# Block 0's first-layer products from unsplit float32 weights and tokens, with the weights split afterwards for block 1

## The chip, the cores and the metric

The kernel runs on one core of one Trainium2 chip. Its time is the device time of one execution in microseconds (us), and versions are compared by the median of several runs on the same chip. The engines carry the names of the profile: PE is TensorE's matmul, PEld its weight load, DVE is VectorE, ACT is ScalarE, POOL is GpSimd, and SP is SyncE, which issues most of the transfers.

## The reference, cut to what matters

Three layers follow one another over 4608 tokens of 512 numbers. The first is attention with 8 batches, 8 heads, 576 queries and keys and values averaged in groups of 8. The second, called the max layer here, is

```python
h = np.maximum(np.maximum(x @ w1, x @ w2), x @ w3)   # 512 -> 768, three weights
y = h @ w_out                                        # 768 -> 512
```

and the third is `h = np.maximum(y @ w_in, 0); out = (h * h) @ w_out` with 2048 hidden units. Everything is float32.

## The kernel before

**Precision.** A float32 operand is written as a sum of two numbers of the type that the profile prints as fp32r, a high part and a low part. `split` makes them: ACT copies the source into the high part (line 135), and a second engine, DVE unless POOL is named, subtracts that from the source and writes the low part (line 136). A product then takes three matmuls for each 128 rows, in the order of `PARTS`: high by high, high by low, low by high. Where an operand is plain float32 the kernel passes it to one matmul as it is; attention does so for the scores (line 367), and for the batch that `NATURAL` counts, batch 0, also for pooling v (line 270) and for the product of probabilities and values (line 426).

**Weights.** The weights come as 64-bit numbers, 512 KB for each 128 by 512 tile. `load_raw` fetches such a tile, `convert` makes float32 bits of it with two ACT instructions (lines 162 and 163) and two DVE instructions (lines 164 and 167) in a tile of the tag `row`, which has three buffers, and `split` with POOL makes the two parts. `weights` does all of it. The max layer has 18 such tiles for its first half (6 slices `f` of the hidden units, 3 weights `e`) and 6 for its second (`wo1`).

**Blocks.** The tokens are taken in 12 blocks of 384. A block of the max layer is 22 steps: 18 products of the first half, four times three matmuls each, and four of the second half. A step yields after its instructions are written down. Attention for block j+1 runs beside the max layer of block j, and attention for blocks 0 and 1 and the preparation of all 24 weight tiles share the start of the kernel. In block 1 the six products of the first `AHEAD` = 2 slices are placed between block 0's last four steps.

**Order.** Everything is put in a list `todo` with a due time in steps, and `run` writes it down in the order of these times. That order gives instructions their priority; a scheduler then fixes each engine's order. An engine takes its instructions strictly in that order. `ps` has three PSUM banks, `hm` (the running maximum) two buffers.

**After block 0.** The second layer's weights are converted and split during blocks 2 to 11, and the third layer follows. None of its code is touched.

Of the kernel before, what the change touches and what calls it, by code (L numbers as in the profile page):

```python
# [11 lines left out]
F32R = mybir.dt.float32r  # L12
I32 = mybir.dt.int32
U32 = mybir.dt.uint32
AF = mybir.ActivationFunctionType
ALU = mybir.AluOpType
# [4 lines left out]
P = 128  # L21
# [6 lines left out]
KD = DM // P  # L28
FF1 = 768
KF1 = FF1 // P  # L30
FF2 = 2048
KF2 = FF2 // P
NE = 3
# [7 lines left out]
PARTS = ((0, 0), (0, 1), (1, 0))  # L41
# [22 lines left out]
AHEAD = 2  # L64
# [21 lines left out]
def as_f32(ap):  # L86
    return ap.bitcast(F32)
# [8 lines left out]
def attention_moe_kernel(ctx: ExitStack, tc: tile.TileContext, q, k, v, vn, w1, w2, w3, wo1, wi2, wo2, out):  # L96
    nc = tc.nc
# [11 lines left out]
    for sign, base in ((1, POOL * MID), (-1, POOL - 1 - POOL * MID)):  # L109
        nc.gpsimd.affine_select(  # L110
            out=sums, in_=sums, compare_op=ALU.is_ge, fill=0.0, base=base,
# [15 lines left out]
    def place(kind):  # L127
        if shared[0]:
            turns["both"] += 1
            return f"raw{turns['both'] % 4}"  # L130
        turns[kind] += 1
        return f"raw{2 * kind + turns[kind] % 2}"

    def split_to(hi, lo, src, engine):
        nc.scalar.activation(hi, src, AF.Copy)  # L135
        engine.tensor_tensor(out=lo, in0=src, in1=as_f32(hi), op=ALU.subtract)  # L136

    def split(hl, src, engine=nc.vector):

        split_to(hl[:, 0], hl[:, 1], src, engine)  # L140

    def load_raw(raw_pool, src, after=None):

        raw = raw_pool.tile([P, 512, 2], I32, tag=place(0), name="wraw", bufs=1)
        if after is not None:
            nc.gpsimd.tensor_copy(as_f32(raw[:1, 0, :1]), after[:1, :1])
        nc.sync.dma_start(out=raw.rearrange("p a b -> p (a b)"), in_=src.bitcast(I32))
        return raw

    def convert(raw_pool, raw, after=None):  # L150

        low, high = raw[:, :, 0], raw[:, :, 1]
        a = raw_pool.tile([P, 512], I32, tag="row", name="wbits", bufs=3)
        if after is not None:  # L160
            nc.gpsimd.tensor_copy(as_f32(a[:1, :1]), after[:1, :1])
        nc.scalar.activation(as_f32(a), as_f32(high), AF.Abs, scale=REBIAS)
        nc.scalar.activation(low, low.bitcast(U32), AF.Copy, scale=LOW_SCALE, bias=LOW_BIAS)  # L163
        nc.vector.scalar_tensor_tensor(
            out=a, in0=a, scalar=3, in1=low, op0=ALU.logical_shift_left, op1=ALU.bitwise_or
        )
        nc.vector.scalar_tensor_tensor(
            out=a, in0=high, scalar=-0x80000000, in1=a, op0=ALU.bitwise_and, op1=ALU.bitwise_or
        )
        return as_f32(a)  # L170

    def in_place(raw):
        return raw.rearrange("p a b -> p (a b)").rearrange("p (c a) -> p c a", c=2).bitcast(F32R)
# [1 line left out]
    def weights(pool, raw_pool, src, name, tag=None):  # L175
        w = pool.tile([P, 2, 512], F32R, name=name, tag=tag or name)
        split(w, convert(raw_pool, load_raw(raw_pool, src)), nc.gpsimd)
        return w


    w_p = s1.enter_context(tc.tile_pool(name="w_p", bufs=1))
# [6 lines left out]
    raw_p = s_at.enter_context(tc.tile_pool(name="raw_p", bufs=4, side="right"))  # L188
# [143 lines left out]
    def attend(j, b, s0, n, p, t):  # L332
# [86 lines left out]
        def values():  # L419
            if t == 0:  # L420
                x_t[j][p] = x_p.tile([P, 2, T1], F32R, tag="x", name="x")
            x = x_t[j][p][:, :, t : t + n]
            if whole:
                av = av_ps.tile([P, T1], F32, tag="av0", name="av0")[:, :n]
                for h in range(2):
                    nc.tensor.matmul(
                        av, lhsT=vst_f[p // 2][:, p % 2, h : h + 2].rearrange("p a d -> p (a d)"), rhs=pt[0][:, h, :n],
                        start=(h == 0), stop=(h == 1),
                    )
                split(x, av)  # L430
                return
            hi, lo = pt[0][:, 0, :, :n], pt[0][:, 1, :, :n]
            xf = xf_p.tile([P, T1], F32, tag="xf", name="xf")[:, :n]
            for h in range(2):
                av = av_ps.tile([P, T1], F32, tag=f"av{h}", name=f"av{h}")[:, :n]
                lhsT = vst[:, p, 2 * h : 2 * h + 2].rearrange("p a d -> p (a d)")
                nc.tensor.matmul(av, lhsT=lhsT, rhs=hi[:, h], start=True, stop=False)  # L437
                nc.tensor.matmul(av, lhsT=lhsT, rhs=lo[:, h], start=False, stop=True)  # L438
                r, o = slice(h * D, (h + 1) * D), slice((1 - h) * D, (2 - h) * D)
                nc.scalar.activation(xf[r], av[o], AF.Copy)  # L440
                nc.vector.tensor_tensor(out=xf[r], in0=av[r], in1=xf[r], op=ALU.add)  # L441
            split(x, xf)

        return load, prepare, softmax, carry, transpose, values

    w1_t, wo1_t = {}, {}

    def load_w1(f, e):
        w1_t[f, e] = weights(w_p, raw_p, (w1, w2, w3)[e][f], f"w1_{f}_{e}")

    def load_second(src, raw):
        raw.append(load_raw(raw_p, src, now[0]))
# [4 lines left out]
    def prepare_out(raw, rows, f):  # L457
# [4 lines left out]
        def store(m, hi, lo):  # L462
            for i, w in enumerate((hi, lo)):
                store_second(wo2_dram[m, g, h][:, u, i], w)

        rows.append(convert(raw_p, raw[0], now[0]))
        own = in_place(raw[0])
        l, r = slice(0, 256), slice(256, 512)
# [58 lines left out]
    now = [None]  # L527

    def moe1(j):

        x = x_t.pop(j)
        hs = []
        for f in range(KF1):
            hm = t_p.tile([P, T1], F32, tag="hm", name="hm")
            h = (ah_p if j == 1 and f < AHEAD else h_p).tile([P, 2, T1], F32R, tag="h", name="h")
            for e in range(NE):
                ps = mm_ps.tile([P, T1], F32, tag="ps", name="ps")
                n = 0
                for kk in range(KD):
                    for a, c in PARTS:  # L540
                        nc.tensor.matmul(  # L541
                            ps, lhsT=w1_t[f, e][:, a, kk * P : (kk + 1) * P], rhs=x[kk][:, c],
                            start=(n == 0), stop=(n == 3 * KD - 1),
                        )
                        n += 1
                if e == 0:
                    nc.scalar.activation(hm, ps, AF.Copy)
                else:
                    nc.vector.tensor_tensor(out=hm, in0=ps, in1=hm, op=ALU.max)  # L549
                if e == NE - 1:  # L550
                    split(h, hm)
                yield
            hs.append(h)
            now[0] = hm
        for d in range(KD):
            ps = mm_ps.tile([P, T1], F32, tag="ps", name="ps")
            n = 0
            for kk in range(KF1):
                for a, c in PARTS:
                    nc.tensor.matmul(  # L560
                        ps, lhsT=wo1_t[kk][:, a, d * P : (d + 1) * P], rhs=hs[kk][:, c],
                        start=(n == 0), stop=(n == 3 * KF1 - 1),
                    )
                    n += 1
            ys = t_p.tile([P, T1], F32, tag="ys", name="ys")
            nc.scalar.activation(ys, ps, AF.Copy)
            nc.scalar.dma_start(out=y_dram[j][d], in_=ys)
            yield
# [6 lines left out]
    def add_moe1(j):  # L575
        steps = moe1(j)
        for i in range(STEPS):
            when = j * STEPS + i
            if j == 1 and i < NE * AHEAD:
                when = NE * KF1 + i * KD / (NE * AHEAD)  # L580
            todo.append((when, functools.partial(next, steps, None)))

    todo = []
    attention(0)
    for f in range(KF1):
        for e in range(NE):
            todo.append((0.9 * (NE * f + e) - 12, functools.partial(load_w1, f, e)))
    for kk in range(KF1):
        todo.append((0.9 * (NE * KF1 + kk) - 12, functools.partial(load_wo1, kk)))
    for j in range(NB1 - 1):  # L590
        add_moe1(j)
        attention(j + 1)

    second = []
    for f in range(0, KF2, 2):
        rows = []
        for i in (f, f + 1):
            raw = []
            second.append((wi2[i], raw, functools.partial(prepare_in, raw, rows, i)))
        rows = []  # L600
        for i in (f // 2 + KF2 // 2, f // 2):
            raw = []
            second.append((wo2[i], raw, functools.partial(prepare_out, raw, rows, i)))
    for i, (src, raw, prepare) in enumerate(second):
        when = STEPS * (SECOND[0] + (i + 0.5) * (SECOND[1] - SECOND[0]) / len(second))
# [236 lines left out]
    for j in range(NB2):  # L842
        for gr in range(NG):
            more = j + 1 < NB2
            c = moe2_in(j, gr)
# [55 lines left out]
```

## Time and profile before

| | |
|---|---|
| median of 3 runs | 1461.22 us (1458.98 to 1462.27) |
| time of the profiled execution | 1462.14 us |
| its span | 1459.7 us |
| PE busy | 1425.5 us, 98% |
| DVE busy | 977.9 us, 67% |
| ACT busy | 759.4 us, 52% |
| POOL busy | 182.9 us, 13% |

The span is the stretch that the trace covers; the 2.4 us around it belong to the time and not to the trace. Busy times are sums over the whole span and hide how unlike its parts are. Only the first 8% or so of the span concerns block 0, and the rows below are therefore taken by stretch. The ends of matmuls are modelled, so PE counts as busy where matmuls follow each other loosely too.

### The profile page before, as it was taken

The numbers are of one execution on the slowest core, as the hardware profiler recorded it, in microseconds if no ns is written. First come the engines' busy times: TensorE is split into PE (matmuls) and PEld (weight loads), VectorE is DVE, ScalarE is ACT, GpSimd is POOL, SyncE is SP. The second block draws the span as 40 slices with busy tenths as digits, with TensorE's granted clock in tenths as the row PEclk, the third lists the DMA queues.
The fourth block names the chain that finished last, engine by engine and source line by source line (L and its number), as shares of the span: only waits on it lengthen the run. The fifth ranks groups of instructions, "written<-read, shape, count | busy, mean of one in ns | idle before, by whom it ended". The sixth has DMA issues, their size and how long they took to land.

```text
span 1459.7 us, 27670 instructions
## 1 busy us (share of the span) xinstructions
PE 1425.5 (98%) x10410; PEld 1403.0 (96%) x10410; DVE 977.9 (67%) x1754; ACT 759.4 (52%) x1959; POOL 182.9 (13%) x229
## 2 busy tenths in 40 slices
PE   6889999999999999999999999999999999999998
PEld 4879999999999999999999999999999999999998
DVE  5887477656675756646336767686867767686865
ACT  7795366655665657655223544453535444454543
POOL 3441022212322222221000000000000000000000
PEclk9989999999999999999999999999999999999999
DMA  7554145444455444433459747566566666555746
GB/s 226 182 169 141 62 143 180 162 140 142 146 180 177 149 148 142 133 120 107 167 190 355 290 160 256 186 223 222 209 221 224 232 231 221 204 217 199 258 153 209
DMA packets 125029, 272.81 MB, mean 187 GB/s; under 512 B 13504, under 2 KB 69568, under 8 KB 124896
## 3 DMA queue, kind: packets, MB, share of 16 engines
q1 hardware_dynamic: 117984, 261.61, 52.8%
q10 hardware_dynamic: 6912, 9.44, 1.8%
q8 instruction: 82, 1.34, 0.4%
q14 instruction: 51, 0.42, 0.1%
HBM read 213.91 MB, written 48.23 MB: 180 GB/s over the span
## 4 chain that ended last, share of the span: by engine, by line
PE 77%; DMA 5%; DVE 2%; ACT 1%; issue 1%; SPq 0%; POOL 0%; ACTq 0%; DVEq 0%; POOLq 0%
PE ps L701 23%; PE ps L541 22%; PE ps L560 8%; PE accB L825 6%; PE accA L825 6%; PE accE L825 3%; PE accF L825 3%; DMA wo2s<-wo_dram 3%; PE accD L825 2%; PE sc L367 2%; PE av L438 1%; PE av L437 1%; DMA wraw<-in_wi_dram 0%; PE tr L408 0%; DMA yr<-y_dram 0%
## 5 line engine op out<-in xcount | busy, mean ns | idle before, releaser
L541 PE MATMUL ps<-x,w 128*128 128x384 f32 x2592 | 491.0, 342 | 5.5 <-ACT w L135 3.0
L541 PEld LDWEIGHTS ps<-x,w 128*128 128x128 f32 x2592 | 452.0, 190 | 8.3 <-ACT w L135 3.4
L701 PE MATMUL ps<-y,wi2s 128*128 128x256 f32 x3024 | 372.8, 278 | 0.7 <-DVE a L672 0.2
L701 PEld LDWEIGHTS ps<-y,wi2s 128*128 128x128 f32 x3024 | 357.2, 188 | 2.4 <-DVE c L672 1.3
L560 PE MATMUL ps<-h,wo 128*128 128x384 f32 x864 | 159.0, 337 | 0.1
L560 PEld LDWEIGHTS ps<-h,wo 128*128 128x128 f32 x864 | 149.6, 188 | 0.3 <-ACT wo L135 0.2
L714 ACT ACTIVATE c<-c 128x512 f32<-128x512 f32 x90 | 56.3, 626 | 168.6 <-DVE c L672 168.0
L672 DVE TENSOR_TENSOR c<-ps,c 128x512 f32<-128x512 f32 x144 | 98.2, 687 | 66.4 <-PE ps L701 63.5
L549 DVE TENSOR_TENSOR hm<-ps,hm 128x384 f32<-128x384 f32 x144 | 79.7, 553 | 81.3 <-PE ps L541 78.8
L135 ACT ACTIVATE g<-c 128x512 fp32r<-128x512 f32 x144 | 90.3, 627 | 57.0 <-DVE c L711 23.3
L825 PE MATMUL accA<-wo2s,g 128*128 128x256 f32 x864 | 115.6, 277 | 0.0
L825 PE MATMUL accB<-wo2s,g 128*128 128x256 f32 x864 | 111.7, 279 | 3.9 <-DMA wo2s<-wo_dram 3.0
L372 ACT ACTIVATE ss<-sc,st 128x72 f32<-128x72 f32 (+1 forms) x320 | 97.8, 320 | 29.9 <-DVE st L369 24.8
L825 PEld LDWEIGHTS accB<-wo2s,g 128*128 128x128 f32 x864 | 104.5, 189 | 4.9 <-ACT g L135 2.2
L136 DVE TENSOR_TENSOR g<-c,g 128x512 fp32r<-128x512 f32 x144 | 97.8, 686 | 16.4 <-ACT g L135 16.4
L825 PEld LDWEIGHTS accA<-wo2s,g 128*128 128x128 f32 x864 | 107.0, 188 | 0.0
L441 DVE TENSOR_TENSOR xf<-av,xf 64x192 f32<-64x192 f32 (+1 forms) x112 | 50.7, 452 | 39.3 <-ACT xf L440 37.6
L378 POOL TENSOR_TENSOR ss<-ss,st 128x432 f32<-128x432 f32 (+1 forms) x64 | 53.1, 830 | 178.3 <-DVE st L377 95.0
L135 ACT ACTIVATE h<-hm 128x384 fp32r<-128x384 f32 x72 | 37.6, 522 | 56.2 <-DVE hm L549 55.5
L372 ACT ACTIVATION_READ_ACCUMULATOR ss<-sc,st 128x1 f32 (+1 forms) x320 | 66.2, 207 | 0.0
L135 ACT ACTIVATE g<-s 128x512 fp32r<-128x512 f32 x72 | 44.3, 630 | 35.3 <-DVE s L675 17.5
L163 ACT ACTIVATE wraw<-wraw 128x512 int32<-128x512 uint32 x56 | 37.8, 675 | 43.4 <-DMA wraw<-in_wi_dram 16.4
(111 smaller groups left out, 1929.2 us busy)
## 6 DMA issues: line engine op xcount, KB each, us to landing
wo2s<-wo_dram SPq DMA_DIRECT2D x252, 512.0 KB, 5.8
wi2s<-wi_dram SPq DMA_DIRECT2D x24, 512.0 KB, 6.5
wraw<-in_wo_dram SPq DMA_DIRECT2D x22, 512.0 KB, 3.9
wraw<-in_w_dram SPq DMA_DIRECT2D x18, 512.0 KB, 5.2
y_dram<-ys ACTq DMA_DIRECT2D x48, 192.0 KB, 2.7
wraw<-in_wi_dram SPq DMA_DIRECT2D x16, 512.0 KB, 3.7
wi_dram<-wraw SPq DMA_DIRECT2D x16, 512.0 KB, 3.0
wo_dram<-wraw SPq DMA_DIRECT2D x64, 128.0 KB, 2.1
```

The source lines that it names most:

```text
L135: nc.scalar.activation(hi, src, AF.Copy)
L136: engine.tensor_tensor(out=lo, in0=src, in1=as_f32(hi), op=ALU.subtract)
L372: nc.scalar.activation(ss[:, i, h], src[:, i, h], AF.Exp, bias=st[:, 0, i, h : h + 1], accum_out=st[:, 1, i, h : h + 1],)
L378: nc.gpsimd.tensor_tensor(out=ss, in0=ss, in1=st[:, 2].rearrange("p g (h o) -> p g h o", o=1).to_broadcast([m, g, 2, SP]), op=ALU.mult,)
L441: nc.vector.tensor_tensor(out=xf[r], in0=av[r], in1=xf[r], op=ALU.add)
L541: nc.tensor.matmul(ps, lhsT=w1_t[f, e][:, a, kk * P : (kk + 1) * P], rhs=x[kk][:, c], start=(n == 0), stop=(n == 3 * KD - 1),)
L549: nc.vector.tensor_tensor(out=hm, in0=ps, in1=hm, op=ALU.max)
L560: nc.tensor.matmul(ps, lhsT=wo1_t[kk][:, a, d * P : (d + 1) * P], rhs=hs[kk][:, c], start=(n == 0), stop=(n == 3 * KF1 - 1),)
L672: nc.vector.tensor_tensor(out=out, in0=in0, in1=in1, op=ALU.add)
L701: nc.tensor.matmul(bank[:, u * HT : (u + 1) * HT], lhsT=wi2_t[2 * gr + u][i][:, a, o + kk * P : o + (kk + 1) * P], rhs=y_t[j][m][:, c, kk] ...
L714: nc.scalar.activation(c, c, AF.Relu)
L825: nc.tensor.matmul(bank[:, i * 256 : (i + 1) * 256], lhsT=g[:, a, u * HT + i * P : u * HT + (i + 1) * P], rhs=w[:, u, c], start=(n == 0 an ...
```

## The change

For block 0 the first half of the max layer is computed with one float32 matmul for each 128 rows, from the converted weights and the unsplit tokens. Block 0's tokens are therefore written once, as float32, by ACT; their subtraction on DVE goes. The converted weight goes straight to a place of its own: two weights share one tile of the size that a split weight has, from the tag `w1_17` downwards, and the last one stays in the `row` buffer. `split_w1` makes the two parts later. It is due behind step 15 for the six weights of the slices 0 and 1, with DVE for the subtraction, and behind step 18 for the other twelve, with POOL. It starts with a copy of one number from the newest `hm` into the target, on POOL, so that the split can't run before that `hm` is final. The targets of the weights 9 to 17 are the tiles that held the unsplit pairs.

```diff
-    def convert(raw_pool, raw, after=None):
+    def convert(raw_pool, raw, after=None, out=None):
...
+        if out is None:
+            out = a
         nc.vector.scalar_tensor_tensor(
-            out=a, in0=high, scalar=-0x80000000, in1=a, op0=ALU.bitwise_and, op1=ALU.bitwise_or
+            out=out, in0=high, scalar=-0x80000000, in1=a, op0=ALU.bitwise_and, op1=ALU.bitwise_or
         )
-        return as_f32(a)
+        return as_f32(out)
...
-                split(x, av)
+                if j == 0:
+                    nc.scalar.activation(as_f32(x[:, 0]), av, AF.Copy)
+                else:
+                    split(x, av)
...
     def load_w1(f, e):
-        w1_t[f, e] = weights(w_p, raw_p, (w1, w2, w3)[e][f], f"w1_{f}_{e}")
+        i = NE * f + e
+        if i == LAST:
+            dst = None
+        else:
+            if i % 2 == 0:
+                two[0] = w_p.tile([P, 2, 512], I32, tag=f"w1_{LAST - i // 2}", name="wf")
+            dst = two[0][:, i % 2]
+        raw = load_raw(raw_p, (w1, w2, w3)[e][f])
+        wf_t[f, e] = convert(raw_p, raw, out=dst)
+
+    def split_w1(f, e):
+        i = NE * f + e
+        half = LAST // 2
+        w1_t[f, e] = w_p.tile([P, 2, 512], F32R, tag=f"w1_{i if i <= half else LAST + half + 1 - i}", name=f"w1_{f}_{e}")
+        nc.gpsimd.tensor_copy(w1_t[f, e][:1, 0, :1], now[0][:1, :1])
+        split(w1_t[f, e], wf_t.pop((f, e)), nc.vector if f < AHEAD else nc.gpsimd)
...
-                    for a, c in PARTS:
-                        nc.tensor.matmul(
-                            ps, lhsT=w1_t[f, e][:, a, kk * P : (kk + 1) * P], rhs=x[kk][:, c],
-                            start=(n == 0), stop=(n == 3 * KD - 1),
-                        )
+                    for a, c in parts:
+                        cols = slice(kk * P, (kk + 1) * P)
+                        if j == 0:
+                            lhsT, rhs = wf_t[f, e][:, cols], as_f32(x[kk][:, c])
+                        else:
+                            lhsT, rhs = w1_t[f, e][:, a, cols], x[kk][:, c]
+                        nc.tensor.matmul(ps, lhsT=lhsT, rhs=rhs, start=(n == 0), stop=(n == len(parts) * KD - 1))
                         n += 1
...
+    for f in range(KF1):
+        for e in range(NE):
+            i = NE * f + e
+            when = NE * (KF1 - 1) if f < AHEAD else NE * KF1
+            todo.append((when + 0.05 * (i + 1), functools.partial(split_w1, f, e)))
```

## Rows read from the trace of the kernel before

**Rows 1.** Busy time of each engine by stretch, granted clock (PEclk, 1.00 is 2.4 GHz).

```profile
28.00:50.00 22.00, 16.36 (x81) 13.20 (x81) 16.80 (x36) 17.47 (x65) 9.33 (x9) 0.88 0.66 194
50.00:75.00 25.00, 24.61 (x153) 23.50 (x152) 22.09 (x46) 19.87 (x69) 12.20 (x11) 1.00 0.57 180
75.00:104.00 29.00, 24.37 (x119) 22.09 (x120) 24.60 (x48) 26.95 (x84) 16.18 (x13) 0.84 0.57 187
104.00:120.00 16.00, 14.82 (x89) 14.22 (x88) 15.41 (x25) 9.80 (x22) 6.42 (x5) 0.97 0.36 113
120.00:135.00 15.00, 15.00 (x93) 14.94 (x91) 8.31 (x18) 9.54 (x40) 1.82 (x2) 1.00 0.57 164
135.00:700.00 565.00, 563.84 (x3487) 560.43 (x3486) 355.22 (x731) 324.24 (x1029) 129.22 (x175) 1.00 0.44 144
```

**Rows 2.** Timeline of PE: start, duration, instructions merged; a dense run and what follows it.

```profile
149.03 10.07 PE L541 MATMUL ps<-x,w 128*128 128x384 f32 x57
158.94 0.53 PE L408 MATMUL tr<-ident,ssr 128*72 128x128 f32 x6
```

**Rows 3.** Timeline of PE, the five float32 matmuls that pool v.

```profile
7.99 5.33 PE L270 MATMUL vp<-natural,sums 128*72 128x512 f32 x10
```

**Rows 4.** Timeline of PEld, weight loads of those matmuls.

```profile
10.44 0.14 PEld L270 LDWEIGHTS vp<-natural,sums 128*72 128x72 f32 x1 [0.29 <-issue]
10.87 0.14 PEld L270 LDWEIGHTS vp<-natural,sums 128*72 128x72 f32 x1 [0.29 <-issue]
```

**Rows 5.** PE groups by line and shape, 28 to 50 us.

```profile
L541 PE MATMUL ps<-x,w 128*128 128x384 f32 x30 | 9.0, 440 | 0.0
L367 PE MATMUL sc<-kbd,qr 128*96 128x144 f32 x24 | 4.8, 328 | 0.3 <-ACT ss L372 0.2
L426 PE MATMUL av<-pt,vst_f 72*128 72x384 f32 x8 | 3.3, 536 | 1.5 <-DVE x L136 1.5
```

**Rows 6.** PE groups by line and shape, 50 to 75 us.

```profile
L541 PE MATMUL ps<-x,w 128*128 128x384 f32 x102 | 20.0, 344 | 0.2 <-ACT hm L547 0.2
```

**Rows 7.** PE groups by line and shape, 75 to 104 us.

```profile
L541 PE MATMUL ps<-x,w 128*128 128x384 f32 x86 | 21.1, 400 | 3.3 <-ACT w L135 3.0 <-POOL w L136 0.3
L367 PE MATMUL sc<-kbd,qr 128*128 128x144 f32 x12 | 1.9, 297 | 0.4 <-ACT ss L372 0.4
L437 PE MATMUL av<-pt,vst 72*128 72x192 f32 x5 | 1.5, 293 | 0.9 <-DVE xf L441 0.9
```

**Rows 8.** Timeline of PE, a transpose of block 1, block 0's last tokens behind it.

```profile
42.30 0.36 PE L408 MATMUL tr<-ident,ss 96*72 96x96 f32 x2 [3.31 <-POOL ss L378]
42.50 1.75 PE L426 MATMUL av<-pt,vst_f 72*128 72x384 f32 x4
```

**Rows 9.** Timeline of ACT, high part of block 0's last token tile.

```profile
46.45 0.49 ACT L135 ACTIVATE x<-av 128x384 fp32r<-128x384 f32 x1
```

**Rows 10.** Timeline of DVE, that tile's low part; last first-half weight's conversion.

```profile
48.96 0.55 DVE L136 TENSOR_TENSOR x<-av,x 128x384 fp32r<-128x384 f32 x1
...
95.25 0.68 DVE L167 SCALAR_TENSOR_TENSOR wbits<-wraw,wbits 128x512 int32<-128x512 int32 x1
```

**Rows 11.** Timeline of PE, first matmul that reads the last first-half weight.

```profile
99.62 0.63 PE L541 MATMUL ps<-x,w 128*128 128x384 f32 x2 [2.24 <-ACT w L135]
```

**Rows 12.** ACT groups, 0 to 125 us: busy, mean ns.

```profile
L135 ACT ACTIVATE w<-wbits 128x512 fp32r<-128x512 f32 x18 | 11.4, 634 | 2.0 <-DVE wbits L167 1.9
```

**Rows 13.** POOL groups of the whole span.

```profile
L136 POOL TENSOR_TENSOR w<-wbits,w 128x512 fp32r<-128x512 f32 x18 | 26.7, 1492 | 21.5 <-ACT w L135 21.5
L146 POOL COPY wraw<-hm 1x1 f32<-1x1 f32 x32 | 6.8, 214 | 39.5 <-DVE hm L549 37.6 <-DMA wi_dram<-wraw 1.3 <-DVE h L136 0.6
```

**Rows 14.** Line 164 alone, 0 to 125 us: shortest, median, longest ns.

```profile
L164 DVE SCALAR_TENSOR_TENSOR wbits<-wbits,wraw x24: 662/685/1870, 19.6 to 113.3; 128x512 int32<-128x512 int32 x24
```

**Rows 15.** DVE groups, 0 to 125 us: busy, mean ns.

```profile
L164 DVE SCALAR_TENSOR_TENSOR wbits<-wbits,wraw 128x512 int32<-128x512 int32 x24 | 21.1, 883 | 6.2 <-ACT wraw L163 2.8 <-ACT wbits L162 2.5 <-issue 0.8
```

More of the change, by code (lines that the diff above doesn't have):

```diff
@@ L444, in attend @@
         return load, prepare, softmax, carry, transpose, values
-    w1_t, wo1_t = {}, {}
+    w1_t, wo1_t, wf_t, two = {}, {}, {}, [None]
+    LAST = NE * KF1 - 1
     def load_w1(f, e):
-        w1_t[f, e] = weights(w_p, raw_p, (w1, w2, w3)[e][f], f"w1_{f}_{e}")
+        i = NE * f + e
[13 more added lines that the diff above has]
+        split(w1_t[f, e], wf_t.pop((f, e)), nc.vector if f < AHEAD else nc.gpsimd)
     def load_second(src, raw):
@@ L537, in moe1 @@
                 ps = mm_ps.tile([P, T1], F32, tag="ps", name="ps")
+                parts = ((0, 0),) if j == 0 else PARTS
                 n = 0
                 for kk in range(KD):
-                    for a, c in PARTS:
-                        nc.tensor.matmul(
-                            ps, lhsT=w1_t[f, e][:, a, kk * P : (kk + 1) * P], rhs=x[kk][:, c],
-                            start=(n == 0), stop=(n == 3 * KD - 1),
-                        )
+                    for a, c in parts:
[5 more added lines that the diff above has]
+                        nc.tensor.matmul(ps, lhsT=lhsT, rhs=rhs, start=(n == 0), stop=(n == len(parts) * KD - 1))
                         n += 1
```

## The prediction

> **What bounds the kernel now.** I read the table of engine times by stretch first [rows 1]. From 120 us on PE has no idle time and the full 2.4 GHz clock, and up to 700 us it idles for 1.2 us of 565. There a microsecond of PE work is a microsecond of the end (what lies behind is not touched), and ACT, DVE and POOL are all far from full. Before 120 us it is another kernel. PE idles for 5.6 us of the 22 from 28 to 50, and for 4.6 us of the 29 from 75 to 104, at a mean clock of 0.88 and 0.84 of full, so part of each stretch ran at 1.2 GHz. Meanwhile ACT is busy for 26.95 us and DVE for 24.60 us of the latter 29. The change acts on just this part. Its effect on the end is therefore one sum: the PE work that it adds, less the PE time that is now lost before 120 us and will not be lost any more, plus whatever loss the moved splits make new.
>
> To use that sum I need prices per matmul. Fifty-seven of the three-part matmuls, 384 columns each, take from 149.03 to 158.94 us: 0.174 us each [rows 2]. Float32 matmuls show as two records each; the five that pool v are ten records [rows 3]. The weight loads of two neighbours start 0.43 us apart for 512 columns at the full clock [rows 4], so 384 columns take 0.3225 us a record and 0.645 us a matmul, and 144 columns 0.121 us a record.
>
> The lost time is the length of a stretch less its matmuls at these prices. From 28 to 50 us the list of PE's groups [rows 5] gives 30 x 0.174 + 24 x 0.121 + 8 x 0.3225 = 10.7 us; the short groups that are left add an estimated 2 us, and 9.3 us of the 22 are lost. From 50 to 75 us the products' 102 matmuls alone take 17.7 us [rows 6], and with 7 us of attention beside them nearly nothing is lost. From 75 to 104 us [rows 7] I get 86 x 0.174 + 12 x 0.121 + 10 x 0.087 = 17.3 us (the ten are five of line 437 and as many of line 438, half as wide as 384 columns), with an estimated microsecond for the rest: some 10.7 us are lost. From 104 to 120 us PE is idle for 1.2 us, and I put the loss at 2 us. Together that is 22 us.
>
> Two waits of PE name the causes. The early loss has one wait of 3.31 us in which a transpose of block 1 stood in PE's queue for POOL; the value product of block 0's last tokens stood right behind it, at 42.50 us [rows 8]. ACT copied those tokens at 46.45 us [rows 9] and DVE finished their low part only at 49.5 us [rows 10]. Until then no product of block 0 can end, and three banks allow only three to be begun. The later loss is that of the weights: the first matmul with the last of the 18 starts at 99.62 us behind ACT's high part [rows 11], although its conversion had ended on DVE at 95.9 us [rows 10].
>
> **The change part by part.**
>
> *PE gains work.* A product had 12 matmuls, 12 x 0.174 = 2.09 us. It now has 4 x 0.645 = 2.58 us. Eighteen products make +8.9 us. The weight loads of 128 columns are not shown for a dense float32 run; at 1.2 GHz the price would double for either kind, which a denser PE makes rarer, and I take the full clock.
>
> *ACT and POOL lose 18 splits before 100 us.* ACT's high parts are 18 x 0.634 = 11.4 us [rows 12], POOL's low parts 18 x 1.49 = 26.7 us [rows 13]. POOL was not full, but its work reaches DVE: line 164, always the same shape, has a median of 685 ns, a longest of 1870 ns [rows 14] and a mean of 883 ns [rows 15], so its 24 instructions lost 24 x 0.198 = 4.8 us. The page SBUF — State Buffer of the Trainium skill (Terms, shared port pair) says that DVE and GpSimd hold one port pair for a whole instruction and that the loser blocks fully; by it up to 18 x 1.49 = 27 us of DVE time would come free, and as much as 12 x 1.49 = 18 us would be blocked again where the twelve late splits land. The longest instruction agrees with one full block, the mean with far fewer. I go on with the 4.8 us of line 164 and as much again for DVE's other instructions, and three quarters of that for the 18 splits out of 24: some 7 us.
>
> *DVE loses four token subtractions*, 4 x 0.55 = 2.2 us [rows 10], and the last tokens are ready when ACT ends, at 46.9 instead of 49.5 us: 2.6 us earlier at once. Some of ACT's high parts lie ahead of that copy too, 0.634 us each. Of the early loss of 9.3 us I take 4 back; the bounds are 1 (another queue order) and 7.
>
> *The weights come earlier.* The last was ready 5 us before POOL's part of it even without relief (95.9 against 101), and ACT and DVE, each 85 to 93% busy [rows 1], have 9 to 11 us less to do ahead of it, so I expect it at 87 to 90 us. PE is then the slower one: from the tokens at about 45 us it has three products to end (1.9 us) and fifteen to make at 2.58 us and some 0.6 us of attention each, 50 us, until 95. The weights stay 5 us ahead, and of the 12 us lost from 50 to 104 I leave 3 for short waits in an order of instructions that I can't see. That gives 9 back; the bounds are 5 and 11.
>
> *The splits come back later.* ACT has the same 11.4 us to do from about step 15 on, DVE six subtractions of the size of line 164's (4.1 us), POOL twelve of 1.49 us and 18 one-number copies of 0.214 us [rows 13], 21.7 us. What hides them: PE needs the slices 0 and 1 first, six products of 2.09 us, and beside them 72 matmuls of the second half, 12.5 us, so the twelve splits on POOL have 25 us before they are wanted, and from 120 to 135 us POOL is busy for 1.8 us of 15, DVE for 8.3 and ACT for 9.5 [rows 1]. On ACT they stand ahead of block 1's later copies, on POOL ahead of the next attention's normalization, but behind all of attention for block 1 and the second-half weights. I cost the return at nothing, with the 2 us of loss from 104 to 120 us kept. If that cover is gone, the price is bounded by DVE: it is busy for 15.41 of these 16 us [rows 1], and 4.1 us plus 12 x 0.25 us of collisions make 7 us. A gain here is bounded by the 2 us.
>
> The sum is 8.9 - 4 - 9 + 0 = -4 us on a span of 1459.7 us, and on the profiled execution's 1462.14 us. That execution is 0.9 us above the median, so beside the median I predict **1457 us**. A measurement of this kernel can tell about 0.2%, 2.9 us, from no change.
>
> **The rivals.**
>
> *More comes back.* With the tokens at 42 us (7 back), 11 us from 50 to 104 and the last 2, the sum is 8.9 - 20 = -11: 1450 us. For it speaks that the 3.31 us wait of the early stretch is an accident of order, and that a denser PE keeps its clock. Against it, every short wait would have to go. Chance 0.14.
>
> *PE pays it back.* The tokens come only 2 us earlier, since their order is set by transfers of k and v, and PE, now the bound, keeps 5 of the 12 us: 8.9 - 2 - 7 = 0, 1461 us. Short waits between engines speak for it. With neighbouring sums within 2.9 us, 0.28.
>
> *The splits return where they hurt, and it is slower.* The one-number copies read the `hm` of block 0's last slice. It has two buffers, and block 1's slice 1 needs the same one. On POOL the twelve copies and subtractions form a chain, since each of the last targets holds an unsplit pair until earlier splits have read it: 12 x 1.7 = 20 us from about 98 us, plus four or so of the second-half subtractions (6 us) and two normalizations (2 us), so the last copy may come as late as 125 us. PE wants the buffer when slice 1's first product is done: 98 us + 25 us of work less some 8 behind it, and two banks more, about 122 us. It decides when the last copy is later than that. With DVE's 7 us above it costs some 9 us: 8.9 - 4 - 9 + 9 = +5, 1466 us. For it speaks that DVE is full to 120 us, against it that second-half subtractions have priority. Chance 0.16.
>
> *The weights don't come earlier.* If the transfers or the four raw places set their pace and not ACT and DVE, 5 of the 12 us come back and 1 of the tokens': +3, 1464 us. Against it, PE's wait for the last weight names ACT [rows 11]. Chance 0.06.
>
> The forecast, 1454 to 1458 us, keeps 0.36. **Faster** by over 0.2% is 0.36 + 0.14 = 0.50, **within** 0.28, **slower** 0.22. The range goes from the first rival's 1450 to beyond the third's 1466: 1449 to 1468 us leaves out the bounds' far ends (8.9 - 20 - 1 and 8.9 - 1 - 5 + 7) and no more than 2 in 10; the forecast's own range is 1453 to 1460.
>
> **What the profile would show.** Right: 72 float32 matmuls in 144 records, 0.32 us apart, for block 0; PE busy and at full clock from about 45 to 95 us; the first matmul with the last weight waiting for PE itself, not for ACT; line 164's mean near 700 ns up to 90 us; the twelve POOL subtractions between 95 and 125 us with no PE wait on `hm` or `ps`; from 125 us on the same order as now. Wrong: float32 records more than 0.33 us apart, a wait of PE on the last tokens beyond 47 us, waits on converted weights, or a gap before 130 us that ends with POOL's copies or ACT's late high parts.

## The result and the profile after

The changed kernel takes 1469.95 us (median of 5 runs, 1467.59 to 1472.20) beside 1460.29 us of the kernel before (5 runs, 1456.75 to 1462.27): a ratio of 1.0066, interval 1.0050 to 1.0081. It is slower by 9.7 us. The prediction had said 1457, with a range that ended at 1468. The profiled execution took 1472.20 us, its span is 1470.5 us. In the code of the changed kernel the products stand in line 568, those of the second half in line 584, and the final conversion in line 169 (line 167 before).

The first view is again that of the engine times by stretch (start and end, length, busy time of PE, PEld, DVE, ACT and POOL, granted clock, DMA share, GB/s); it answers to [rows 1].

```profile
28.00:50.00 22.00, 19.34 (x82) 13.02 (x81) 17.62 (x44) 16.83 (x69) 4.18 (x6) 0.89 0.77 239
50.00:75.00 25.00, 25.00 (x101) 16.22 (x100) 19.50 (x42) 17.09 (x48) 2.26 (x3) 0.99 0.60 205
75.00:95.00 20.00, 19.84 (x79) 12.50 (x77) 14.70 (x29) 17.22 (x53) 6.54 (x7) 1.00 0.62 196
95.00:105.00 10.00, 4.57 (x23) 3.59 (x21) 10.00 (x15) 6.23 (x15) 6.73 (x8) 0.83 0.46 122
105.00:125.00 20.00, 17.14 (x81) 15.98 (x82) 13.58 (x29) 15.26 (x52) 16.34 (x23) 0.75 0.35 108
125.00:140.00 15.00, 15.00 (x90) 14.67 (x89) 4.61 (x10) 6.62 (x23) 5.12 (x6) 1.00 0.12 42
```

From 50 to 95 us PE is full and at full clock, as forecast. From 95 to 105 us it is busy for less than half of the time, with DVE busy for all of it, and from 105 to 125 us its mean clock is 0.75, so a good part of that stretch ran at 1.2 GHz. The same two stretches of the kernel before:

```profile
95.00:105.00 10.00, 7.69 (x36) 7.23 (x35) 7.56 (x16) 9.48 (x30) 4.93 (x5) 0.83 0.48 159
105.00:125.00 20.00, 18.82 (x120) 18.16 (x118) 17.23 (x30) 13.91 (x41) 5.97 (x4) 1.00 0.40 121
```

PE's timeline of the changed kernel shows the dense part and what comes behind it.

```profile
52.45 6.61 PE L568 MATMUL ps<-x,wf 128*128 128x384 f32 x20
...
92.56 2.85 PE L568 MATMUL ps<-x,wbits 128*128 128x384 f32 x8 [0.15 <-DVE hm L573]
95.15 2.38 PE L584 MATMUL ps<-h,wo 128*128 128x384 f32 x12
97.37 0.65 PE L369 MATMUL sc<-kbd,qr 128*128 128x144 f32 x4
100.65 0.62 PE L584 MATMUL ps<-h,wo 128*128 128x384 f32 x2 [2.63 <-ACT wo L135]
101.11 0.41 PE L369 MATMUL sc<-kbd,qr 128*128 128x144 f32 x2
104.05 0.69 PE L584 MATMUL ps<-h,wo 128*128 128x384 f32 x1 [2.54 <-POOL wo L136]
105.06 1.33 PE L568 MATMUL ps<-x,w 128*128 128x384 f32 x3 [0.33 <-DVE hm L573]
107.38 0.51 PE L410 MATMUL tr<-ident,ss 96*72 96x96 f32 x2 [0.99 <-DVE xf L446]
```

The twenty records from 52.45 us end where the next instruction starts, at 58.91: 0.323 us each. Block 0's first half ends at 95.1 us, and then PE stands for second-half weights (`wo`) that ACT and POOL have not split yet. DVE's timeline of these microseconds says why all is late at once.

```profile
97.88 0.68 DVE L136 TENSOR_TENSOR w<-wf,w 128x512 fp32r<-128x512 f32 x1
...
100.82 1.28 DVE L136 TENSOR_TENSOR w<-wf,w 128x512 fp32r<-128x512 f32 x2
102.02 0.68 DVE L169 SCALAR_TENSOR_TENSOR wbits<-wraw,wbits 128x512 int32<-128x512 int32 x1
102.62 0.74 DVE L243 TENSOR_REDUCE ks<-kr 128x72 f32<-128x576 f32 x1
103.28 1.26 DVE L136 TENSOR_TENSOR w<-wf,w 128x512 fp32r<-128x512 f32 x1
104.47 0.54 DVE L573 TENSOR_TENSOR hm<-ps,hm 128x384 f32<-128x384 f32 x1
104.93 0.59 DVE L371 TENSOR_REDUCE st<-sc 128x6 f32<-128x432 f32 x1
105.45 1.39 DVE L136 TENSOR_TENSOR w<-wf,w 128x512 fp32r<-128x512 f32 x2
106.87 0.36 DVE L446 TENSOR_TENSOR xf<-av,xf 64x192 f32<-64x192 f32 x1
```

The six late subtractions (`w<-wf`) stand between the last conversions and the `xf` addition for block 1's second token tile, whose other half ACT had written at 99.73 us:

```profile
99.41 0.32 ACT L445 ACTIVATE xf<-av 64x192 f32<-64x192 f32 x1
```

It waited 7 us in DVE's queue. Five of the six subtractions passed there in that time, 3.9 us in the rows above; the rest of the wait is conversions, reductions and block 0's own steps. On POOL a part of a second-half weight meets the same subtractions, and the rest of the late splits follows.

```profile
100.67 5.01 POOL L136 TENSOR_TENSOR wo<-wbits,wo 128x512 fp32r<-128x512 f32 x2 [3.27 <-ACT wo L135]
108.15 0.77 POOL L469 CAST w<-hm 1x1 fp32r<-1x1 f32 x6 [2.46 <-DVE hm L573]
109.26 5.91 POOL L136 TENSOR_TENSOR w<-wf,w 128x512 fp32r<-128x512 f32 x4 [0.34 <-ACT w L135]
```

So the last tokens of block 1, which PE needs for all products of its next block, are finished by DVE at 122.7 us, in the kernel before at 111.1 us. First the changed kernel, then the one before.

```profile
122.23 0.49 DVE L136 TENSOR_TENSOR x<-xf,x 128x192 fp32r<-128x192 f32 x1
```

```profile
110.71 0.35 DVE L136 TENSOR_TENSOR x<-xf,x 128x192 fp32r<-128x192 f32 x1
```

Further back a second wait has grown, in attention for a later block; PE's timeline of the changed kernel, then of the one before:

```profile
244.93 0.51 PE L401 MATMUL tr<-ident,ssr 96*72 96x96 f32 x4 [2.12 <-DMA ssr<-ss]
245.23 3.75 PE L568 MATMUL ps<-x,w 128*128 128x384 f32 x12
```

```profile
237.13 0.39 PE L399 MATMUL tr<-ident,ssr 96*72 96x96 f32 x4 [0.37 <-DMA ssr<-ss]
237.36 2.34 PE L541 MATMUL ps<-x,w 128*128 128x384 f32 x12
```

The twelve matmuls behind the wait take 3.75 us instead of 2.34.

**Where the time went.** I count lost PE time as the prediction did, length less all matmuls at its prices (0.174 us for 384 columns of a part, 0.3225 us for a float32 record of 384, other widths in proportion; a record counts where it starts), summed from the start of the span. "Added" is the PE work that a version adds in block 0; the last but one column is that plus the loss to 260 us less the 42.3 of the kernel before; the last is the version's profiled execution less the 1462.14 us of the kernel before. Both are of one execution, and not of the medians. E1, E3, E11 and E14 are experiments told below.

| | lost to 95 us | to 125 us | to 260 us | added | sum | profiled |
|---|---|---|---|---|---|---|
| before | 33.5 | 40.0 | 42.3 | 0 | 0 | 0 |
| changed | 21.7 | 36.3 | 42.4 | 8.9 | +9.0 | +10.1 |
| E1 | 24.6 | 34.2 | 40.2 | 8.9 | +6.8 | +5.0 |
| E3 | 30.8 | 37.3 | 41.0 | 9.4 | +8.1 | +8.9 |
| E11 | 22.7 | 33.4 | 39.8 | 8.9 | +6.4 | +6.9 |
| E14 | 30.0 | 38.8 | 42.1 | -2.8 | -3.0 | -2.5 |

The changed kernel gains 11.8 us to 95 us. From 95 to 125 us it loses 14.6, where the kernel before loses 6.5, and from 125 to 260 us 6.1, where that loses 2.3. By 260 us it has kept nothing: what is left is the added work of PE.

### The profile page after: what moved, and what is told of

It reads as the page before. It is cut to its first block, busy times and chain, and to the rows that moved or that the text cites. A ratio compares the mean times of both kernels' runs of the same rounds, so it can differ in the third digit from the quotient of the medians.

```text
span 1470.5 us, 27550 instructions
## 1 busy us (share of the span) xinstructions
PE 1434.5 (98%) x10338; PEld 1393.4 (95%) x10338; DVE 973.0 (66%) x1756; ACT 759.3 (52%) x1959; POOL 177.1 (12%) x241
## 4 chain that ended last, share of the span: by engine, by line
PE 59%; DMA 4%; issue 1%; DVE 1%; ACT 1%; POOL 0%; SPq 0%; POOLq 0%; ACTq 0%; DVEq 0%
PE ps L730 22%; PE ps L568 10%; PE accB L854 7%; PE accA L854 6%; PE ps L584 4%; PE accE L854 3%; DMA wo2s<-wo_dram 3%; PE accF L854 3%; PE accD L854 2%; PE sc L369 1%; PE av L443 0%; DMA wraw<-in_wi_dram 0%; PE av L442 0%; ACT ss L374 0%; PE tr L410 0%
## 5 line engine op out<-in xcount | busy, mean ns | idle before, releaser
L568 PE MATMUL ps<-x,w 128*128 128x384 f32 x2376 | 445.3, 339 | 0.4 <-DVE hm L573 0.3
L568 PEld LDWEIGHTS ps<-x,w 128*128 128x128 f32 x2376 | 412.5, 189 | 1.1 <-DVE hm L573 1.1
L445 ACT ACTIVATE xf<-av 64x192 f32<-64x192 f32 (+1 forms) x112 | 45.4, 405 | 34.8 <-PE av L443 25.8
```

The costliest lines, as they stand in the source:

```text
L568: nc.tensor.matmul(ps, lhsT=lhsT, rhs=rhs, start=(n == 0), stop=(n == len(parts) * KD - 1))
```

## The experiments

Each ratio is against the kernel before on the same chip. From the trace I had two theories: that the returning splits cost the time (A in the expectations), by the DVE queue above, by POOL's run, or by the `row` buffer that the last unsplit weight holds; and, against it, that PE's added work itself is paid, since attention for block 1, on which PE then waits, passes PE behind block 0's products (D in the last expectations). The other letters: B says only that PE's added work is not hidden; C that attention for block 1 stands on ACT, DVE and POOL behind conversions and splits; P that POOL's run of subtractions shuts out DVE. Experiments stand here by what they tell; their numbers are in the order in which they ran.

**E13, the changed kernel once more**, beside the last group of runs, no edit.

> The changed kernel itself once more, as the base of this group: ratio 1.005 to 1.008 to the kernel before if the first measurement holds, and the profile's loss by stretch as before (block 0's first half ends near 95 us, block 1's last tokens near 122 us).

1472.16 us, 1.0055 (1.0042 to 1.0067). With the first result the change costs about 0.6%, 8.8 us. In its trace block 1's last tokens end at 125.7 us, not near 122 as expected.

**E1, the splits don't come back.** Block 1 onwards uses one split weight for all 18; the last unsplit weight moves to the tile of a weight that is left out.

```diff
-            dst = None
+            dst = w_p.tile([P, 2, 512], I32, tag="w1_1", name="wf")[:, 0]
...
+        if i:
+            w1_t[f, e] = w1_t[0, 0]
+            return
```

> Leaves out 17 of the 18 late splits: blocks 1 to 11 read the split of the first weight in place of all 18, and the last unsplit weight lies in a free weight tile, not in a row buffer. All matmuls stay. Theory A (the late splits on ACT, DVE and POOL, and the row buffer that the last weight holds, delay the second-half weights and block 1's tokens between 95 and 125 us, a new loss of 8 to 9 us): 8 to 10 us faster than the changed kernel, about 1460 us, with under 4 us lost from 95 to 125 us. Theory B (the extra PE work of 8.9 us is simply not hidden): within 2 us of the changed kernel's 1470 us.

1465.69 us, 1.0015 (1.0000 to 1.0030). By the ratios the return of the splits costs 0.6 - 0.15 = 0.45%, some 6.6 us (4 to 9 with both intervals), not nothing, and by the median less than theory A's 8 to 10; 9.6 us are still lost from 95 to 125 us, where A wanted under 4. The edit also frees the `row` buffer, so the 6.6 us are not the splits' alone. But without it the change still gains nothing: the forecast's own terms, 8.9 - 4 - 9, would have made it 4 us faster. Block 1's last tokens are as late as in the changed kernel (ACT writes them at 121.2 us).

**E2, the last unsplit weight elsewhere**, in a buffer of the second half's `h`, so that the three `row` buffers are free for the second-half weights.

```diff
-            dst = None
+            dst = ah_p.tile([P, 2, T1], I32, tag="h", name="wf").rearrange("p a t -> p (a t)")[:, :512]
```

> The changed kernel, with the last unsplit weight in one of the two h buffers that block 0 leaves empty, so that the second-half weights have three row buffers again. Theory A1 (the row buffer is what delays the second-half weights, which are converted in pairs): 4 to 6 us faster than the changed kernel, the waits of PE for the second-half weights at 100 and 104 us gone. Theory A2 (the splits' own work on ACT, DVE and POOL does it): within 2 us of the changed kernel. Theory B: no change.

1479.26 us, 1.0112 (1.0092 to 1.0133): slower still, so the time doesn't say what the `row` buffer is worth. The traces do show what it delays. PE's two waits for second-half weights in the changed kernel, 2.6 and 2.5 us, are gone here, as in E1 and E9, which free that buffer too; E10 to E13, which don't, have both. (E14 frees the buffer and waits 3.9 us once, but its first half ends at 85.2 us instead of 95.1.) In the changed kernel ACT begins the fifth of these conversions only when POOL has let go of a buffer, and the sixth behind it:

```profile
93.52 0.68 ACT L162 ACTIVATE wbits<-wraw 128x512 f32<-128x512 f32 x1 [0.45 <-POOL wo L136]
94.99 0.69 ACT L162 ACTIVATE wbits<-wraw 128x512 f32<-128x512 f32 x1
```

What took the place of these waits in E2 stands in DVE's timeline, and POOL's beside it:

```profile
110.34 7.50 DVE L136 TENSOR_TENSOR h<-hm,h 128x384 fp32r<-128x384 f32 x1
```

```profile
110.02 7.41 POOL L136 TENSOR_TENSOR w<-wf,w 128x512 fp32r<-128x512 f32 x6
```

A DVE subtraction that takes 0.54 us elsewhere stood still for the whole run of six late subtractions on POOL, and PE waited 5.0 us for its `h`.

**E3, the kernel before with 9.4 us more PE work in block 0** and nothing else: 54 matmuls of 0.174 us repeat one of a product's parts.

```diff
-                    for a, c in PARTS:
+                    for a, c in PARTS + (((0, 1),) if j == 0 and kk else ()):
```

> The kernel before, with 15 three-part matmuls instead of 12 in each first-half product of block 0 (the low token part is added once more for three of four row groups): 18 x 3 x 0.174 = 9.4 us more PE work and nothing else. Theory B: 9 us slower than before. The prediction's ground (PE has 22 us to spare before 120 us, while it waits for tokens and weights): 1 to 4 us slower.

1470.39 us, 1.0046 (1.0029 to 1.0063), 6.7 us (4.2 to 9.2): more than the 1 to 4 of the prediction's ground and less than the 9 of theory B. DVE ends block 1's last tokens 12 us later than before, with no split moved:

```profile
122.79 0.36 DVE L136 TENSOR_TENSOR x<-xf,x 128x192 fp32r<-128x192 f32 x1 [0.16 <-ACT x L135]
```

PE idles before 120 us in this kernel [rows 1], and yet some 70% of the work that was added there is paid. This is the step on which the prediction's sum stands.

**E4, the changed kernel with three of the four float32 matmuls** of each product, 18 x 0.645 = 11.6 us less PE work.

```diff
-                for kk in range(KD):
+                rows = (0, 2, 3) if j == 0 else range(KD)
+                for kk in rows:
```

> The changed kernel, with three of the four float32 matmuls in each first-half product of block 0 (one row group is left out): 18 x 0.645 = 11.6 us less PE work ahead of 95 us, all else as in the changed kernel. Theory B: 11 to 12 us faster than the changed kernel. Theory A: block 0's first half ends up to 10 us earlier, but second-half weights and block 1's tokens still come late, so under 6 us of it reach the end.

1478.27 us, 1.0100 (1.0081 to 1.0119): less work, and slower. The trace has the shut-out of E2 again, on DVE and on POOL:

```profile
95.27 10.45 DVE L164 SCALAR_TENSOR_TENSOR wbits<-wbits,wraw 128x512 int32<-128x512 int32 x1
```

```profile
95.59 0.90 POOL L380 TENSOR_TENSOR ss<-ss,st 128x432 f32<-128x432 f32 x1
96.46 6.15 POOL L136 TENSOR_TENSOR w<-wf,w 128x512 fp32r<-128x512 f32 x5
102.56 0.17 POOL L469 CAST w<-hm 1x1 fp32r<-1x1 f32 x1
102.70 1.25 POOL L136 TENSOR_TENSOR w<-wf,w 128x512 fp32r<-128x512 f32 x1
103.92 1.25 POOL L136 TENSOR_TENSOR wo<-wbits,wo 128x512 fp32r<-128x512 f32 x1
```

PE waited 11.4 us for the `xf` addition behind that conversion. The run told nothing of PE's work; E14 repeats it without the splits.

**E14, E1 and E4 together**: three of four matmuls, and no splits that come back.

> The run without late splits (e1), with three of the four float32 matmuls in each first-half product of block 0: 11.6 us less PE work, and no run of subtractions on POOL that could shut out DVE as it did in e4. Theory D (block 1's tokens pass PE several times, behind block 0's products, so PE work in block 0 delays them and is paid at the end): tokens at 112 us or earlier instead of 122, and 6 to 9 us under e1, below the kernel before. Theory C (ACT, DVE and POOL alone set them): within 3 us of e1.

1459.38 us, 0.9970 (0.9958 to 0.9982): 0.45%, 6.6 us, under E1 for 11.6 us less PE work. Block 1's last tokens come 11.7 us earlier than in E1 (121.62 us there):

```profile
109.94 0.36 DVE L136 TENSOR_TENSOR x<-xf,x 128x192 fp32r<-128x192 f32 x1 [0.94 <-ACT x L135]
```

E3 and E14 say the same with opposite signs: some 60 to 70% of PE work in block 0 reaches the end (each share within some 25 points, by the intervals), by way of the time at which block 1's tokens are ready.

**E5 and E8, attention for block 1 placed earlier** (its pace in steps shortened), in the changed kernel and in the one before.

```diff
-BRISK = 0.7
+BRISK = 0.5
```

> The changed kernel with BRISK = 0.5 instead of 0.7: attention for block 1 is due earlier, ahead of more of the weights' preparation. In the changed kernel the last first-half weight is converted at 78 us and read at 92 us, while block 1's last tokens come at 122.7 us. Theory C (what block 1 waits for is attention for block 1, which passes ACT, DVE and POOL in queues behind conversions and splits that are early): block 1's tokens earlier by 5 us or more, the time 3 to 8 us under the changed kernel's 1470 us. Theory A (the late splits): within 2 us of the changed kernel.

> A control for e5: the kernel before with BRISK = 0.5. There the weights come just in time and PE waits for them, so putting attention for block 1 ahead of them should cost time: 0 to 5 us slower than before (Theory C as well as A).

E5: 1474.63 us, 1.0080 (1.0055 to 1.0104); E8: 1471.78 us, 1.0061 (1.0041 to 1.0080). Neither is faster. In E5 DVE's timeline has

```profile
111.38 8.00 DVE L136 TENSOR_TENSOR h<-hm,h 128x384 fp32r<-128x384 f32 x1
```

beside a POOL run of six, and PE waited 7.7 us for it, so the run doesn't say what earlier attention is worth; E8 says that in the kernel before it costs 0.6%, some 9 us, more than the 0 to 5 expected.

**E6, the splits wait for block 1's last tokens** instead of the newest `hm`.

```diff
-        nc.gpsimd.tensor_copy(w1_t[f, e][:1, 0, :1], now[0][:1, :1])
+        nc.gpsimd.tensor_copy(w1_t[f, e][:1, 0, :1], as_f32(tokens[NPAIR - 1][:1, 0, T1 - 1 :]))
```

> The changed kernel, with every late split made to wait for block 1's last tokens instead of the newest hm, so that no split can stand ahead of attention for block 1. Theory A: DVE's six subtractions no longer delay the sum of attention's halves (7 us in the changed kernel), and most of the 7 us that the run without late splits gained comes back: 4 to 7 us under the changed kernel. Theory C alone: within 3 us of it, since the queues are full of conversions anyway; and block 1's first products can then be late by the 1 to 2 us of a split.

1479.90 us, 1.0117 (1.0086 to 1.0147). ACT writes the tokens 4 us earlier than in the changed kernel, but DVE's six subtractions now run from 119.5 to 124.3 us. The products that the changed kernel begins at 105.06 us, on block 1's first token tiles, have no split weight here until PE's timeline shows

```profile
119.53 1.65 PE L572 MATMUL ps<-x,w 128*128 128x384 f32 x4 [0.55 <-ACT w L135]
```

and PE is nearly out of work ahead of it, busy for 8.0 of the 14.5 us from 105 us at a clock of 0.50. The gain of 4 to 7 us that theory A expected is a loss: what the splits cost isn't saved by putting them behind the tokens.

**E7, all late subtractions on POOL.**

```diff
-        split(w1_t[f, e], wf_t.pop((f, e)), nc.vector if f < AHEAD else nc.gpsimd)
+        split(w1_t[f, e], wf_t.pop((f, e)), nc.gpsimd)
```

> The changed kernel with all 18 late subtractions on POOL (six were on DVE). Theory A, DVE's queue: block 1's tokens 4 us earlier, the time 3 to 5 us lower. If POOL's run of subtractions is the harm (DVE's instructions with two SBUF inputs stood still beside it for 7.5 us in one run and 10.5 us in another): 2 us or more slower than the changed kernel. Theory C: within 2 us.

1477.86 us, 1.0099 (1.0073 to 1.0125). Two conversions on DVE take 9.3 us from 97.95 us on, beside six POOL subtractions from 98.71 to 106.07, and PE waits 9.2 us for a second-half weight.

**E9 to E12, which of the late splits cost.** E9 leaves out the twelve, E10 five of the six on DVE (as E1 does, for those weights alone). E11 and E12 leave nothing out: the twelve are due one per step instead of all behind step 18, on POOL or on DVE.

```diff
-            when = NE * (KF1 - 1) if f < AHEAD else NE * KF1
-            todo.append((when + 0.05 * (i + 1), functools.partial(split_w1, f, e)))
+            when = NE * (KF1 - 1) + 0.05 * (i + 1) if f < AHEAD else NE * KF1 + i
+            todo.append((when, functools.partial(split_w1, f, e)))
```

> The changed kernel without the twelve late splits of the slices 2 to 5, which run on ACT and POOL (blocks 1 to 11 read the first weight's split for them; the last unsplit weight lies in a free weight tile). The six on ACT and DVE stay. Theory A (DVE's six stand ahead of attention for block 1): within 2 us of the changed kernel. Theory P (the run of subtractions on POOL, which shuts out DVE's instructions with two SBUF inputs, does the harm): 5 to 8 us under the changed kernel, like the run without late splits.

> The changed kernel without five of the six late splits of the slices 0 and 1 (blocks 1 to 11 read the first weight's split for them). The twelve on ACT and POOL stay. Theory A: 4 to 7 us under the changed kernel. Theory P: within 2 us of it, or above it.

> The changed kernel with the twelve late splits on POOL due one per step of block 1, four steps ahead of their product, instead of all behind step 18. Nothing is left out. Theory P: no run of POOL subtractions before 125 us, so the time falls by 4 to 7 us, to about 1463 to 1466 us. Theory A: within 2 us of the changed kernel.

> As e11, with all late subtractions on DVE, 0.69 us each instead of 1.3 to 1.5 us on POOL. Theory P: as e11 or 1 to 2 us better, since POOL has no late subtraction at all; DVE is busy for half the time by then. Theory A: no better than the changed kernel.

E9: 1469.57 us, 1.0042 (1.0028 to 1.0056). E10: 1469.45 us, 1.0038 (1.0024 to 1.0053). E11: 1468.77 us, 1.0033 (1.0019 to 1.0046). E12: 1470.63 us, 1.0041 (1.0026 to 1.0055). Beside the changed kernel's 0.6%, which was not run on this chip, either group costs about 0.2% of the 0.45, and spreading the twelve on POOL takes 0.27% away without leaving anything out; each of these differences has an interval of nearly 0.2% either way. E9 frees the `row` buffer as well. Neither group explains the whole by itself, as theories A and P had it.

**E15 and E16, float32 only for the last slices of block 0**, slices 4 and 5 in E15, slice 5 in E16; the other weights are split ahead as before. The tokens exist in both forms, unsplit ones in buffers of `h`.

```diff
+                single = j == 0 and f >= FIRST    # FIRST = 4 in E15, 5 in E16
+                parts = ((0, 0),) if single else PARTS
...
+                        if single:
+                            lhsT, rhs = wf_t[f, e][:, cols], whole_x[kk // 2][:, kk % 2]
```

> Float32 products for the slices 4 and 5 of block 0 alone, six of 18, where PE lost 10.7 us in the kernel before; the first twelve weights are split on loading as before, block 0's tokens are kept both split and whole (the whole ones in the empty h buffers), and the six late splits are due one per step of block 1. 3.0 us of PE work come in, 3.8 us of ACT and 9 us of POOL go out from 75 to 100 us. If the extra PE work is paid only where PE is full: 1 to 5 us faster than before. Theory D: it is paid there too, within 2 us of before or up to 3 us slower.

> As e15 for slice 5 alone, three of 18 products: 1.5 us of PE work in, half of the relief. Half of e15's difference to before, within 2 us of it either way.

E15: 1465.01 us, 1.0011 (0.9998 to 1.0025). E16: 1468.95 us, 1.0031 (1.0019 to 1.0042). With a third of the added PE work and six late splits E15 is level with the kernel before. E16 adds half of that and is slower, which neither theory explains. Both write block 0's tokens a third time, on ACT, and PE waits 4.7 us (E15) and 4.1 us (E16) for those tokens' low parts on DVE, 2.0 us in the kernel before; that may be a part of it, which no run shows. No version that computes everything beats the kernel before.

## Why the prediction was wrong

*Prices: right; the bound: nearly.* From 125 to 140 us PE is busy throughout. But by the table the changed kernel loses 3.8 us more than the kernel before between 125 and 260 us, where the prediction had "the same order as now". A float32 record of 384 columns takes 0.323 us (0.3225 forecast), so PE gains 8.9 us.

*Relief of DVE: right in the main.* The view of line 164 alone, 0 to 125 us, and its group in the changed kernel answer to [rows 14, 15]:

```profile
L164 DVE SCALAR_TENSOR_TENSOR wbits<-wbits,wraw x24: 657/684/1353, 19.1 to 98.5; 128x512 int32<-128x512 int32 x24
```

```profile
L164 DVE SCALAR_TENSOR_TENSOR wbits<-wbits,wraw 128x512 int32<-128x512 int32 x24 | 17.1, 717 | 6.7 <-ACT wraw L163 6.0 <-ACT wbits L162 0.4
```

The mean fell from 883 to 717 ns, 4.0 us over the 24. The second conversion (line 167, now 169) fell from 18.2 to 16.6 us; that makes 5.6 of the "some 7 us".

*Tokens and weights earlier: they are, and by more than forecast.* ACT ends block 0's last tokens at 39.6 us (46.9 forecast, 49.5 before), and DVE the last first-half weight at 78.2 us (87 to 90 forecast, 95.9 before); no product waits for a weight, and block 0's first half ends at 95.1 us as forecast. The rows, of ACT and of DVE:

```profile
39.08 0.50 ACT L433 ACTIVATE x<-av 128x384 f32<-128x384 f32 x1
```

```profile
77.49 0.68 DVE L169 SCALAR_TENSOR_TENSOR wbits<-wraw,wbits 128x512 int32<-128x512 int32 x1
```

*"That gives 9 back", with the 4 of the tokens: wrong in size.* The working itself slips here: its rows gave 10.7 us lost from 75 to 104 and nearly nothing from 50 to 75, and it went on with 12, so that 9 should have been 8 at most. The larger fault is that the loss that goes before 95 us comes again behind it. With no splits coming back (E1) the ratio gives +2.2 us, so of the 13 only 8.9 - 2.2 = 6.7 were kept; in the changed kernel nothing of them is left by 260 us, as the table shows. The step that failed is the sum itself: PE time that is lost before 120 us was taken as free to fill. Behind block 0's first half PE has 12.5 us of second-half products, and then needs block 1's tokens. These come from attention, whose scores, transposes and value products stand in PE's queue behind block 0's products; each product is now 2.58 us long instead of 2.09, and the tokens move with them. Runs show the tokens' shift and its price; the way through PE's queue is read from the kernel's order. E3 has both with PE work alone (tokens 12 us later, 6.7 us paid of 9.4), E14 in reverse (11.7 us earlier, 6.6 us gained of 11.6).

*"I cost the return at nothing": wrong.* It costs 6.6 us by E1, the `row` buffer included, near the 7 that the text gave for a lost cover. The cover was counted on engines' mean load and for PE's need of the weights, but the late subtractions were placed ahead of the rest of attention for block 1: six on DVE, then full from 95 to 105 us, with a token addition 7 us behind them, and the first of the twelve on POOL from 109 us on. "Behind all of attention for block 1 and the second-half weights" was the false premise. It holds for the due times: attention for block 1 is due by step 9, the first late split behind step 15. But due times are only priorities, and the scheduler's order on DVE has five of the six ahead of that addition.

With both, -4 becomes 8.9 - 6.7 + 6.6 = +8.8 us. This meets the 8.8 us by construction, since both terms come from E1's ratio; E3 and E14 are the independent tests of the first. How the 8.8 us divide is not well known: in the single executions of the table E1 keeps 2.1 us and not 6.7, and lies only 2.2 us under the changed kernel to 260 us, 5.1 us in the whole time. Either step alone would have made it slower by less than 0.2%, 2.9 us: with the return at 6.6 and 13 back, the sum is +2.5, and with the return at nothing and 6.7 back, +2.2. The prediction's own far bounds, 1 for the tokens, 5 for the weights and 7 for the splits, sum to 8.9 - 1 - 5 + 7 = +9.9 us, about what was measured; the range left that end out.

*The rivals.* The third had the sign and one half of its mechanism: DVE was full. The other half, a PE wait for the `hm` buffer that POOL's copies hold, isn't there: from 90 to 125 us no step on `hm` waits for POOL, and PE's longest wait that a step on `hm` ends is 0.33 us. The second had the right idea of a PE that pays back, without its cause: its tokens come only 2 us earlier, and here they came 10 us earlier. The first and the fourth are refuted, for nothing is gained and the weights did come earlier.

**Open.** What the `row` buffer costs at the end, apart from the splits, no run shows. The wait of 2.1 us near 245 us is there with 1.4 to 2.3 us in the changed kernel, E1, E3, E11, E13 and E15, whose block 1 tokens are ready between 118.4 and 125.7 us, and is 0.4 us in the kernel before (111.1 us) and 1.0 us in E14 (110.3 us). But E16, ready at 118.7 us, has 0.3 us of it, so late tokens alone don't decide it, and its cause stays open, with that of the 3.8 us behind 125 us. Each edit also lets the scheduler set the order of all engines anew; E2, E5 and E16 hold such a part that I can't separate.

## What to carry to other kernels

Idle time of an engine in a start phase is free only if nothing that ends the idleness passes that same engine: follow what it waits for back, and if the chain goes through its own queue, work that is put into the gap moves the end of the gap. A step that is moved to "where the engines have room" must be placed by the queue it lands in, and by what stands behind it there, not by busy shares or by its due time. Adding the same work to the old kernel (E3) tests such a sum by itself.

## What the runs showed of the hardware

A DVE instruction with two SBUF inputs can stand still through a whole run of POOL instructions, and not only through one of them: 7.50 us (E2) and 8.00 us (E5) beside six subtractions, 10.45 us (E4) beside the run shown there, where the same instructions take 0.54 to 0.68 us. PE waited 5.0, 7.7 and 11.4 us behind them. It isn't always so: in the changed kernel the same `h` subtraction ran in 0.54 us at 109.78 us, inside a POOL run of four. The other way round, POOL's pair from 100.67 us on, beside DVE's late subtractions in the changed kernel, took up to 3.32 us for one, where E4's rows have 1.25 (shortest, median, longest ns of line 136 on POOL, 100 to 106 us):

```profile
L136 POOL TENSOR_TENSOR wo<-wbits,wo x2: 1757/2539/3321, 100.7 to 103.9; 128x512 fp32r<-128x512 f32 x2
```

The page SBUF — State Buffer of the Trainium skill (Terms, shared port pair) says that the loser blocks for the other's full instruction. The stops agree in kind; a stop that lasts through six POOL instructions (7.41 us in E2) is more than the page states. Such stops spoiled E2, E4, E5 and E7.
